# A scan with a mixture of adapters behind it: transposes over 128 rows in place of pairs over 64

## The chip, the cores and the metric

The kernel runs on one core of one Trainium2 chip. The time is the device time of one execution in microseconds; three runs of the kernel before give a median of 207.19 us (206.95 to 208.16). A profile is one execution, taken by the hardware profiler on that core, with every instruction of the five engines (PE, the tensor engine with its weight loads PEld; DVE, the vector engine; ACT, the scalar engine; POOL; SP, which here only issues DMAs) and every DMA packet.

## What is computed

```python
for t in range(S):                      # _attn_ref: a, b are [8, 6400, 128] float32
    h = a[:, t] * h + b[:, t]
    out[:, t] = h
...
logits = x @ w_gate                     # _moe_ref: x is out as [51200, 128]; 8 experts, rank 16
topk = np.argpartition(-logits, K, axis=1)[:, :K]   # K = 2
sel = np.take_along_axis(logits, topk, axis=1)
w = softmax(sel)
for e, k: delta[mask] += w[mask, k, None] * ((x[mask] @ A[e]) @ B[e])
return x + delta
```

A first-order recurrence runs over the tokens, separately for each of 128 channels. Each resulting row then goes through a mixture of eight small adapters, of which the two with the highest logits count.

## The kernel before, in words

The 51200 tokens are cut into 100 chunks of 512 (C = 512, NCH = 100, J = C/128 = 4). A chunk passes through a front and, later, a back.

**Front.** `load` (L526) brings a and b of a chunk with the tokens on the partitions. `front` (L582) transposes them on PE against a float32 identity into PSUM (`trans`, L557, issues at L562), so that the channels lie on the partitions and time along the row: a into `pA`, b into `pB`, two banks each. ACT copies a from PSUM to `a_st` (`add_ae`, L580). DVE runs the recurrence as one TENSOR_TENSOR_SCAN per chunk (L613), reads a_st and pB, and writes the states as float16 to `xT`, of which 24 buffers exist.

**Logits and adapters' first half.** For a unit of six 128-token blocks (`zlogits`, L624) PE multiplies xT by A and w_gate together (L633) into `pZ`, and ACT copies the result to `zl` (L639). **Gating** (`gating`, L645) works on four units, that is six chunks, at once: DVE finds the two largest logits and POOL does the elementwise steps; the last six smaller groups (WIDE_DVE) have all of it on DVE.

**Back** (`back`, L693). zl is multiplied by the gates into `zw`, on POOL at L707 (`mu`) or, for the chunks counted from the end in MU_DVE, on DVE at L711 (`md`). PE transposes zw (L720, float16), the result is copied to `zwT` on DVE (L729) or ACT (L726; `te_act`, L505, chooses), PE adds x and zwT times B in PSUM `pO` (L734 with the identity, L735 with B), ACT copies to `outt` (L744), and `store` (L769) sends two chunks at a time, 512 KB, to HBM. For the last twelve chunks `place` (L752) lets the back use pA and pB too.

**Two kinds of loads.** The first eight chunks (HEAD = 8) come as loads of 256 KB each: a partition gets four tokens, a contiguous 2 KB. `front` transposes such a chunk with four transposes of 128 rows for a (operation A) and four for b (operation B). From chunk 8 on, `paired` (L523) is true: one load of 512 KB brings two chunks, a partition gets eight contiguous tokens, 4 KB, so the first chunk of the pair lies on partitions 0 to 63 and the second on 64 to 127. A chunk's transposes are then over 64 rows, eight per tensor (`pieces`, L547):

```python
dv = dst.rearrange("d (p j) -> d j p", j=HC * J)
lo, hi = 64 * h, 64 * h + 64
return [(dv[:, j, :], t[lo:hi, j, :], ident_f[lo:hi, lo:hi]) for j in range(HC * J)]
```

To use both halves of the array, one operation P joins two such sets on different halves, a of one chunk with b of its neighbour, and alternates them (L592, L597): P of 16 transposes waits for a load of a and a load of b, and for a free bank of each. The load tiles `a_tm` and `b_tm` have six slots of two chunks each.

**Order.** Nothing is a loop at run time. `Program` (L176) gets every operation with an engine, a duration estimate, its dependences and a rank (base by chunk, TEMPLATE by kind, NUDGE by name). `schedule` (L208) simulates the five queues with constants for rates and delays and picks, per engine, from the operations within WINDOW ranks of the first one the one that can start earliest. `waits` (L278) then derives the semaphore waits from the order. All loads but one (b of chunk 0, on ACT) and all stores are issued from SP, in one queue. SPLIT sends two stores (chunks 56 and 78) as two DMAs of 120 and 8 partitions.

Of the kernel before, what the change touches and what calls it, by code (L numbers as in the profile page):

```python
# [15 lines left out]
PE_FREE = 0.1  # L16
Q_RATE = {3: 3.6e-3, 5: 2.1e-3, 7: 2.1e-3}
SCAN_SELF = 0.13
ISSUE = {"sp": 0.52, "act": 0.45}
LOAD_RATE = 392e3  # L20
STORE_RATE = 408e3
# [86 lines left out]
START = (-999, "", 0)  # L108
FIRST = -9999
EARLY = -400  # L110
LEAD = []
TAPER = [2, 2, 1, 1, 1, 1]
WIDE_DVE = [1, 2, 3, 4, 5, 6]
TE_LAST = []
TAIL_UNITS = [4, 4, 4, 4]
TE_ACT = [1]
MU_DVE = [1, 2, 4, 6, 8]
TAIL_CHUNKS = 12
WARM0 = 12
WARM = 16  # L120
HALVES = 0.745
PAIR_RATE = 411e3
HEAD = 8
TAIL = 0
STORE_TAIL = [1, 1, 1, 1]
# [754 lines left out]
```

## Time and profile before

| | us |
|---|---|
| median of three runs | 207.19 (206.95 to 208.16) |
| the profiled execution | 207.91 |
| its span, first to last instruction | 205.9 |
| mean granted clock of PE, share of full | 0.975 |
| DMA: moved, mean over the span | 79.26 MB, 385 GB/s |

The page names a group of instructions by line, engine, operation, and its output and inputs; "x24" is a count, followed by busy us and mean ns of one, then the idle us of the engine just before them and what ended it. In a shape like 64*128 64x64 f32 the first part is the weights' active rows and columns, the second the moving operand. The table by stretch gives the busy us of each engine in each window of time and the number of its instructions there. Matmuls are pipelined, so 0.22 us is the time of one from start to end, and the distance between starts is what it costs in a stream. The groups that the change touches hold, for the whole span:

| group | count, mean ns |
|---|---|
| transposes of 64 rows, L562 | 736 into pA, 736 into pB, 232 each |
| transposes of 128 rows, L562 | 32 into pA, 298; 32 into pB, 290 |
| loads of 512 KB, 4 KB rows | 46 of a, 46 of b; 10.7 and 10.6 us from issue to landing |
| loads of 256 KB, 2 KB rows | 8 of a, 7 of b on SP and 1 on ACT |
| stores of 512 KB, 2 KB rows | 46 |

### The profile page before, as it was taken

How to read it: one execution, taken by the hardware profiler on the slowest of the kernel's cores; microseconds unless marked ns; L12 is line 12 of the kernel's file. 1: busy time of each engine (PE TensorE's matmuls, PEld its weight loads, DVE VectorE, ACT ScalarE, POOL GpSimd, SP SyncE). 2: the span in 40 equal slices, each digit the busy share in tenths (PEclk: the TensorE clock that was granted, in tenths of full speed). 3: DMA queues.
4: the chain of work that ended last, by engine and by line, in shares of the span. 5: the costliest groups of instructions: out<-in, count | busy, mean ns of one | idle time of the engine just before them, and what ended most of it. 6: DMA issues, size and time to landing. Idle time of an engine off the chain costs nothing.

```text
span 205.9 us, 7539 instructions
## 1 busy us (share of the span) xinstructions
PE 184.7 (90%) x3152; PEld 160.9 (78%) x3152; DVE 177.7 (86%) x289; ACT 169.1 (82%) x306; POOL 144.6 (70%) x176
## 2 busy tenths in 40 slices
PE   7779589999998899899799999999999999879683
PEld 6557478887897789788689888988888888857572
DVE  0789688998998899798899999999997999989881
ACT  2356668999998999899799999999999998886372
POOL 1000328879898978878788988899989898687420
PEclk9999958999999999999999999999999999999789
DMA  6999999999999999999999999999999999997388
GB/s 191 368 392 415 405 409 406 405 409 405 411 417 406 414 403 417 409 403 416 408 409 400 409 395 408 415 410 411 409 412 410 410 409 404 405 352 289 132 299 300
DMA packets 30559, 79.26 MB, mean 385 GB/s; under 512 B 3774, under 2 KB 3902, under 8 KB 30526
## 3 DMA queue, kind: packets, MB, share of 16 engines
q1 hardware_dynamic: 29054, 78.39, 97.1%
q10 hardware_dynamic: 1472, 0.40, 0.8%
q8 instruction: 25, 0.41, 0.8%
q14 instruction: 8, 0.07, 0.1%
HBM read 52.56 MB, written 26.21 MB: 383 GB/s over the span
## 4 chain that ended last, share of the span: by engine, by line
PE 67%; DVE 12%; DMA 10%; POOL 3%; issue 3%; SPq 2%; ACT 1%; DVEq 0%; POOLq 0%
PE pA L562 14%; PE pB L562 12%; PE pZ L633 11%; PE pO L734 10%; PE pO L720 10%; PE pO L735 9%; DMA a_tm<-in_a_dram 7%; DVE xT L613 5%; DMA b_tm<-in_b_dram 3%; POOL zw L707 3%; SPq L541 2%; DVE zwT L729 2%; DVE zw L711 1%; ACT outt L744 1%; DVE g L688 1%
## 5 line engine op out<-in xcount | busy, mean ns | idle before, releaser
L613 DVE TENSOR_TENSOR_SCAN xT<-a_st,xT,pB 128x512 f16<-128x512 f32 x96 | 120.3, 1253 | 9.5 <-PE pA L562 5.6
L707 POOL TENSOR_TENSOR zw<-zl,g 128x512 f16<-128x512 f32 x95 | 100.4, 1069 | 24.7 <-PE pO L720 11.3
L562 PE MATMUL pB<-ident_f,b_tm 64*128 64x64 f32 (+1 forms) x768 | 71.4, 235 | 6.5 <-DMA a_tm<-in_a_dram 2.8
L580 ACT COPY a_st<-pA 128x512 f32<-128x512 f32 x100 | 60.5, 612 | 17.5 <-PE pA L562 16.0
L562 PE MATMUL pA<-ident_f,a_tm 64*128 64x64 f32 (+1 forms) x768 | 71.7, 235 | 2.0 <-DMA a_tm<-in_a_dram 1.0
L562 PEld LDWEIGHTS pB<-ident_f,b_tm 64*128 64x128 f32 (+1 forms) x768 | 57.9, 142 | 12.5 <-issue 3.7
L562 PEld LDWEIGHTS pA<-ident_f,a_tm 64*128 64x128 f32 (+1 forms) x768 | 57.9, 142 | 8.2 <-DMA a_tm<-in_a_dram 2.3
L639 ACT COPY zl<-pZ 128x816 f32<-128x816 f32 (+1 forms) x68 | 58.0, 853 | 2.3 <-PE pZ L633 1.6
L744 ACT COPY outt<-pO 128x512 f32<-128x512 f32 x92 | 52.7, 609 | 7.7 <-PE pO L735 7.3
L734 PE MATMUL pO<-ident_h,xT 128*128 128x128 f16 x368 | 50.1, 223 | 1.2 <-DVE zwT L729 1.0
L735 PE MATMUL pO<-cst_h,zwT 128*128 128x128 f16 x368 | 48.9, 220 | 0.8 <-issue 0.8
L734 PEld LDWEIGHTS pO<-ident_h,xT 128*128 128x128 f16 x368 | 40.5, 114 | 4.8 <-DVE zwT L729 2.1
L633 PE MATMUL pZ<-cst_h,xT 128*128 128x136 f16 x400 | 36.5, 228 | 1.5 <-DVE xT L613 0.6
L735 PEld LDWEIGHTS pO<-cst_h,zwT 128*128 128x128 f16 x368 | 36.9, 100 | 0.8 <-issue 0.8
L720 PE MATMUL pO<-ident_h,zw 128*128 128x128 f16 x368 | 33.2, 221 | 2.0 <-ACT outt L744 1.3
L729 DVE COPY zwT<-pO 128x512 f16<-128x512 f16 x77 | 30.2, 410 | 3.4 <-PE pO L720 3.1
L633 PEld LDWEIGHTS pZ<-cst_h,xT 128*128 128x128 f16 x400 | 27.1, 115 | 4.4 <-DVE xT L613 1.3
L720 PEld LDWEIGHTS pO<-ident_h,zw 128*128 128x128 f16 x368 | 22.3, 98 | 6.0 <-issue 1.9
L669 POOL TENSOR_TENSOR k<-zl,m 128x192 f32<-128x192 f32 x15 | 7.8, 519 | 22.9 <-DVE m L667 22.9
L671 POOL TENSOR_SCALAR L<-k 128x192 f32<-128x192 f32 x15 | 12.9, 860 | 1.3
L613 DVE TENSOR_TENSOR_SCAN xT<-a_st,pB 128x512 f16<-128x512 f32 (+1 forms) x8 | 7.5, 939 | 4.6 <-PE pB L562 4.3
L678 POOL TENSOR_TENSOR L<-k,m 128x192 f32<-128x192 f32 x15 | 7.9, 524 | 2.8 <-DVE m L676 2.7
(41 smaller groups left out, 106.1 us busy)
## 6 DMA issues: line engine op xcount, KB each, us to landing
a_tm<-in_a_dram SPq DMA_DIRECT2D x46, 512.0 KB, 10.7
b_tm<-in_b_dram SPq DMA_DIRECT2D x46, 512.0 KB, 10.6
out_dram<-outt SPq DMA_DIRECT2D x46, 512.0 KB, 10.8
a_tm<-in_a_dram SPq DMA_DIRECT2D x8, 256.0 KB, 5.8
b_tm<-in_b_dram SPq DMA_DIRECT2D x7, 256.0 KB, 6.0
out_dram<-outt SPq DMA_DIRECT2D x4, 256.0 KB, 2.7
out_dram<-outt SPq DMA_DIRECT2D x2, 480.0 KB
b_tm<-in_b_dram ACTq DMA_DIRECT2D x1, 256.0 KB, 3.6
```

The costliest lines, as they stand in the source:

```text
L562: last = eng["pe"].transpose(*args)
L580: lambda: eng["act"].copy(a_st[c % NA][:, :], pA[:, c % 2, :]), fr(c, "ae"))
L613: last = eng["dve"].tensor_tensor_scan(out=x[:, s0:s1], data0=a_st[c % NA][:, s0:s1], data1=pB[:, c % 2, s0:s1], initial=init, op0=ALU.mul ...
L633: last = eng["pe"].matmul(pZ[:, k // (n // 2), o : o + W], xblock(b0 + k), Awg_h)
L639: return eng["act"].copy(zl[:, zb : zb + n, :].rearrange("p (h k) w -> p h (k w)", h=2), pZ[:, :, 0 : n // 2 * W])
L671: lambda e: e.tensor_scalar(out=ll, in0=kk, scalar1=0.0, scalar2=-1.0e30, op0=ALU.is_ge, op1=ALU.mult), dve=not main)
L707: lambda: eng["pool"].tensor_tensor(out=wv, in0=zv, in1=gv, op=ALU.mult), ba(gi, c, "mu"))
L720: last = eng["pe"].transpose(ptile[:, k * 128 : k * 128 + 128], zw[w][:, k, :], ident_h[:, :])
L729: lambda: eng["dve"].tensor_copy(zwT[w][:, :], ptile[:, 0:C]), ba(gi, c, "te"))
L734: eng["pe"].matmul(dst, xblock(b0 + k), ident_h[:, :], start=True, stop=False)
L735: last = eng["pe"].matmul(dst, zwT[w][:, k * 128 : k * 128 + 128], B_h, start=False, stop=True)
L744: lambda: eng["act"].copy(outt[:, o0 : o0 + n, :].rearrange("p k w -> p (k w)"), bank),
```

## The change

HEAD goes from 8 to 4, and a new list FLAT names the pairs 2 to 49, that is every chunk from 4 on. `paired` is false for them. Their loads are still 512 KB for two chunks, but arranged as the single ones were: each partition gets four tokens of the first chunk and four of the second, two runs of 2 KB. So every chunk lies on all 128 partitions, and every chunk is transposed as the first eight were: four transposes of 128 rows for a (operation A) and four for b (operation B), as separate operations with waits of their own. No P operation is left. In the tail, MU_DVE goes from five of the last eight chunks to all of the last ten, so five more products move from POOL to DVE; TE_LAST, empty before, names six of the last ten chunks whose zwT copy moves from DVE to ACT. SPLIT becomes empty, so no store is cut. All ranks are new (TEMPLATE, NUDGE, WINDOW), the planner's rates are slightly different, and it counts two margins for the order alone: 2.0 us for what SP waits for and 1.0 us behind a DMA.

```diff
-LOAD_RATE = 392e3
-STORE_RATE = 408e3
+SP_MARGIN = 2.0
+LAND_MARGIN = 1.0
+LOAD_RATE = 387e3
+STORE_RATE = 413e3
...
-WINDOW = {'pe': 16.262, 'act': 17.153, 'dve': 47.02, 'pool': 47.064, 'sp': 57.831}
+WINDOW = {'pe': 70.239, 'act': 22.0, 'dve': 48.055, 'pool': 40.461, 'sp': 37.357}
...
-TE_LAST = []
+TE_LAST = [1, 2, 4, 6, 8, 10]
+HEAD_UNITS = []
+FLAT = [2, 3, 4, ..., 49]
-MU_DVE = [1, 2, 4, 6, 8]
+MU_DVE = [1, 2, 3, 4, 5, 6, 7, 8, 9, 10]
-PAIR_RATE = 411e3
-HEAD = 8
+PAIR_RATE = 414.5e3
+HEAD = 4
-SPLIT = {56: [120, 8], 78: [120, 8]}
+SPLIT = {}
...
+    def margin(self, d, op):
+        return (SP_MARGIN if op.eng == "sp" else 0.0) + (LAND_MARGIN if d.sem is not None else 0.0)
...
-                users[d.i].append((op, self.lag(d, op)))
+                users[d.i].append((op, self.lag(d, op) + self.margin(d, op)))
...
         def paired(c):
-            return HEAD <= c < NCH - TAIL
+            return HEAD <= c < NCH - TAIL and c // HC not in FLAT
...
-                    q, f"{key}{c}", n * C * D * 4 / (PAIR_RATE if paired(c) else LOAD_RATE),
+                    q, f"{key}{c}", n * C * D * 4 / (PAIR_RATE if paired(c) else STORE_RATE if n == HC else LOAD_RATE),
```

The NUDGE and TEMPLATE tables, all of whose numbers differ, are left out, as are changes that have no effect with these settings (HEAD_UNITS is empty).

More of the change, by code (lines that the diff above doesn't have):

```diff
@@ L113 @@
 WIDE_DVE = [1, 2, 3, 4, 5, 6]
-TE_LAST = []
+TE_LAST = [1, 2, 4, 6, 8, 10]
 TAIL_UNITS = [4, 4, 4, 4]
+HEAD_UNITS = []
+FLAT = [2, 3, 4, 5, 6, 7, 8, 9, 10, 11, 12, 13, 14, 15, 16, 17, 18, 19, 20, 21, 22, 23, 24, 25, 26, 27, 28, 29, 30, 31, 32, 33, 34, 35, 36, 37, 38, 39, 40, 41, 42, 43, 44, 45, 46, 47, 48, 49]
 TE_ACT = [1]
-MU_DVE = [1, 2, 4, 6, 8]
+MU_DVE = [1, 2, 3, 4, 5, 6, 7, 8, 9, 10]
 TAIL_CHUNKS = 12
@@ L121 @@
 HALVES = 0.745
-PAIR_RATE = 411e3
-HEAD = 8
+PAIR_RATE = 414.5e3
+HEAD = 4
 TAIL = 0
 STORE_TAIL = [1, 1, 1, 1]
-SPLIT = {56: [120, 8], 78: [120, 8]}
+SPLIT = {}
 TEMPLATE = {
-    "la": [-13.284, -13.376, -10.147],
-    "lb": [-12.856, -11.393, -13.112],
-    "A": [3.619, 4.619, -4.264, 6.619, 7.619, 8.619],
-    "B": [-2.245, 2.718, -8.407, 8.99, 6.061, 4.41],
-    "ae": [-1.493, 12.357, 10.831, 7.96, 5.931, 11.772],
-    "sc": [-2.149, -1.286, 6.521, -19.69, -9.638, -0.216],
-    "Z": [6.623, 2.916, -2.696, 9.959],
-    "ze": [6.413, 12.686, 18.636, 4.611],
-    "g1": [1.078],
-    "g2": [15.192],
-    "g3": [12.311],
-    "g4": [-7.624],
-    "g5": [43.586],
-    "g6": [18.91],
-    "w1": [27.261],
+    "la": [-17.155, -9.476, -8.608],
+    "lb": [-13.364, -10.414, -12.68],
+    "A": [16.518, 7.296, 8.525, 9.015, 10.156, 14.759],
+    "B": [6.922, 7.465, 8.658, 10.963, 11.979, 21.937],
+    "ae": [-7.077, -3.484, 19.127, 16.938, 8.043, 17.193],
+    "sc": [12.365, 35.856, 12.744, 17.786, 39.079, 14.296],
+    "Z": [-3.119, 5.335, 10.342, 12.093],
+    "ze": [8.877, 13.518, 17.919, 16.392],
+    "g1": [12.118],
+    "g2": [-0.105],
+    "g3": [10.708],
+    "g4": [15.86],
+    "g5": [12.078],
+    "g6": [28.459],
+    "w1": [12.393],
     "w2": [27.183],
@@ L146 @@
     "p3": [35.473],
-    "mu": [22.377, 11.789, 38.051, -6.995, 25.901, 25.822],
-    "T": [17.564, 18.694, 15.643, 19.013, 20.568, 20.925],
-    "te": [11.47, 21.167, 12.791, -1.785, 1.996, 11.732],
-    "D": [13.525, 17.402, 15.169, 14.035, 19.652, 27.901],
-    "oe": [26.926, 32.894, 33.316, 36.556, 35.829, 26.06],
-    "st": [25.679, 26.621, 29.881],
-    "ta": [14.725, 30.746, 16.943, 18.052, 19.161, 20.27],
-    "md": [78.718, -0.018, -87.87, 12.1, 13.209, 14.318],
+    "mu": [-6.716, -6.575, 22.528, 27.11, 24.647, 25.876],
+    "T": [22.12, 19.993, 15.194, 8.772, -12.047, 12.625],
+    "te": [11.32, 58.704, 8.268, 34.31, 22.158, 22.327],
+    "D": [21.417, 22.577, 2.823, -5.791, 8.081, -5.073],
+    "oe": [23.904, 20.839, 22.806, 31.415, 27.39, 36.64],
+    "st": [23.265, 25.145, 26.221],
+    "ta": [17.267, 11.772, 45.843, 23.351, 24.128, 24.904],
+    "md": [3.609, 47.296, 8.162, 22.686, 23.463, 24.239],
     "wu": [-0.198],
-    "ch": [26.813],
+    "ch": [-35.18],
     "mb": [0.0],
-    "q2": [17.668],
-    "q3": [-16.399],
-    "q5": [-0.842],
-    "q6": [-2.93],
-    "q7": [1.928],
+    "q2": [-17.861],
+    "q3": [-7.73],
+    "q5": [3.392],
+    "q6": [14.473],
+    "q7": [-2.223],
     "q8": [35.473],
-    "g7": [47.426],
-    "g8": [9.111],
+    "g7": [15.59],
+    "g8": [17.3],
 }
@@ L348, in bass_associative_scan_2x2__then__mixture_of_adapters_kernel @@
     b0 = 0
-    for n in [U] * ((NBLK - sum(TAIL_UNITS)) // U) + TAIL_UNITS:
+    for n in HEAD_UNITS + [U] * ((NBLK - sum(HEAD_UNITS) - sum(TAIL_UNITS)) // U) + TAIL_UNITS:
         units.append((b0, n))
@@ L513, in un @@
         def un(u, kind):
-            return (PERIOD * (u // GMAX), kind, u % GMAX)
+            v = u - len(HEAD_UNITS)
+            if v < 0:
+                return ((units[u][0] + units[u][1] - 1) // J - 1, kind, 0)
+            return (sum(HEAD_UNITS) // J + PERIOD * (v // GMAX), kind, v % GMAX)
         def ga(gi, kind):
@@ L721, in tr @@
                 return last
-            o_T[c] = P.add("pe", f"T{c}", 0.1 + 0.056 * n, [(o_mu[c], True), (o_ih, True)] + free + [(o, True) for o in o_wu if c < 2], tr, ba(gi, c, "T"))
+            o_T[c] = P.add("pe", f"T{c}", 0.1 + 0.056 * n, [(o_mu[c], True), (o_ih, True)] + free + [(o, True) for o in (o_wu if c < 2 else [])], tr, ba(gi, c, "T"))
             if te_act(c):
```

159 rows, old and new, of the table NUDGE are left out of this document.

## The prediction

> **What bounds the kernel now.** I read the page first: its busy shares, its 40 slices and its chain.
>
> ```profile
> span 205.9 us, 7539 instructions
> PE 184.7 (90%) x3152; PEld 160.9 (78%) x3152; DVE 177.7 (86%) x289; ACT 169.1 (82%) x306; POOL 144.6 (70%) x176
> PE   7779589999998899899799999999999999879683
> DVE  0789688998998899798899999999997999989881
> PEclk9999958999999999999999999999999999999789
> DMA  6999999999999999999999999999999999997388
> PE 67%; DVE 12%; DMA 10%; POOL 3%; issue 3%; SPq 2%; ACT 1%; DVEq 0%; POOLq 0%
> ```
>
> DMA is full from 5 to about 187 us, yet the chain that ended last runs through PE for 67% of the span and through DMA for 10%. So the transfers are busy but early; the compute engines, PE ahead, pace the middle. How tightly, the table by stretch says (busy us of PE, PEld, DVE, ACT, POOL; then clock, DMA share, GB/s), with the row of the tile pA alone (PE, PEld, DVE, ACT) under it:
>
> ```profile
> 30.00:180.00 150.00, 144.14 (x2679) 127.27 (x2677) 139.41 (x210) 139.33 (x252) 129.76 (x155) 0.99 1.03 409
> 162.20:172.20 10.00, 10.00 (x196) 8.96 (x194) 9.65 (x15) 9.63 (x18) 9.61 (x12) 1.00 1.04 411
> 180.00:190.00 10.00, 8.25 (x121) 6.71 (x119) 8.94 (x30) 7.24 (x15) 7.47 (x8) 1.00 0.89 332
> 190.00:200.00 10.00, 7.69 (x97) 6.91 (x94) 8.35 (x31) 5.29 (x14) 3.62 (x3) 0.83 0.53 197
> ...
> 30.00:180.00 150.00, 60.08 (x672) 48.83 (x672) 0.00 (x0) 50.17 (x83) 0.99 1.03 409
> ```
>
> The last row counts 83 evacuations of a on ACT in 150 us: one chunk per 1.81 us. In the second row PE has no gap; the groups of PE in that stretch show what a chunk costs it there:
>
> ```profile
> L562 PE MATMUL pA<-ident_f,a_tm 64*128 64x64 f32 x48 | 4.3, 229 | 0.0
> L734 PE MATMUL pO<-ident_h,xT 128*128 128x128 f16 x24 | 3.4, 222 | 0.0
> ```
>
> 48 half transposes of a, eight to a chunk, are six chunks in 10 us (and 24 matmuls with ident_h, four to a chunk, are six as well): 1.67 us each when PE runs without a gap, against 1.81 on average. PE has a few per cent of slack in the middle, no more.
>
> **The change, part by part.** *1. Transposes over 128 rows.* Every chunk from 8 on loses 16 transposes of 64 rows and gets 8 of 128 rows. The timeline of PE shows one paired operation between its neighbours (start, duration), and, from the first 20 us, transposes over 128 rows:
>
> ```profile
> 162.25 0.52 PE L633 MATMUL pZ<-cst_h,xT 128*128 128x136 f16 x6
> 162.60 0.22 PE L734 MATMUL pO<-ident_h,xT 128*128 128x128 f16 x1
> ...
> 162.99 0.22 PE L735 MATMUL pO<-cst_h,zwT 128*128 128x128 f16 x1
> 163.14 0.27 PE L562 MATMUL pA<-ident_f,a_tm 64*128 64x64 f32 x1
> ...
> 163.63 0.22 PE L562 MATMUL pA<-ident_f,a_tm 64*128 64x64 f32 x1
> 163.79 0.55 PE L633 MATMUL pZ<-cst_h,xT 128*128 128x136 f16 x6
> ```
>
> ```profile
> 10.01 0.60 PE L562 MATMUL pA<-ident_f,a_tm 128*128 128x128 f32 x4
> 10.86 0.66 PE L562 MATMUL pB<-ident_f,b_tm 128*128 128x128 f32 x4 [0.25 <-DMA b_tm<-in_b_dram]
> 16.85 0.55 PE L633 MATMUL pZ<-cst_h,xT 128*128 128x136 f16 x6
> 17.23 0.39 PE L483 MATMUL pO<-ident_f 128*128 128x128 f32 x2
> ```
>
> Paired: D's eight matmuls start from 162.60 to 162.99, a step of 0.39/7 = 0.056 us, but from the last of them to the first half transpose (163.14) it is 0.15, so entering costs 0.095. From 163.14 to the next operation at 163.79 it is 0.65. Together 0.745 us per chunk. Over 128 rows: four last 0.60 us and the last of them 0.27, so the step is 0.33/3 = 0.11 and a tensor's four take 0.437 (0.109 each before rounding); two tensors 0.874. The difference is +0.129 us per chunk, the lower end if A and B enter for nothing. Entering is not quite free: six logits matmuls that step to D in 0.35 (162.25 to 162.60) step to a 128-row f32 transpose in 0.38 (16.85 to 17.23), and a group that had waited takes 0.66 instead of 0.60. With 0.03 for each of the two visits it is +0.19, the upper end. Which visits follow one another the trace of before cannot show; I take +0.15, nearer the lower end because A and B stand side by side or follow a ready neighbour when PE is the late engine.
>
> [...]
>
> *The middle, 30 to 180 us.* The clock around its start, by stretch, and PE's work in it by groups:
>
> ```profile
> 22.60:26.00 3.40, 1.68 (x38) 1.45 (x38) 1.63 (x2) 1.57 (x4) 1.98 (x3) 1.00 1.02 408
> 26.00:33.00 7.00, 6.54 (x82) 5.49 (x82) 5.67 (x8) 4.96 (x8) 3.04 (x4) 0.51 1.03 408
> ```
>
> ```profile
> L562 PE MATMUL pB<-ident_f,b_tm 64*128 64x64 f32 x680 | 60.5, 230 | 2.3 <-issue 2.0
> L562 PE MATMUL pA<-ident_f,a_tm 64*128 64x64 f32 x672 | 60.1, 231 | 0.9 <-issue 0.9
> L734 PE MATMUL pO<-ident_h,xT 128*128 128x128 f16 x324 | 43.4, 222 | 0.4 <-DVE zwT L729 0.3
> L633 PE MATMUL pZ<-cst_h,xT 128*128 128x136 f16 x353 | 31.7, 226 | 0.6 <-DVE xT L613 0.3
> L720 PE MATMUL pO<-ident_h,zw 128*128 128x128 f16 x326 | 29.0, 220 | 0.8 <-POOL zw L707 0.5 <-ACT outt L744 0.2
> ```
>
> By steps: 1352/16 = 84.5 chunks x 0.745 = 63.0; L734 with L735 (as many), 648 x 0.0557 = 36.1; L633, 353 x 0.35/6 = 20.6; L720, of the same shape as L734, 326 x 0.0557 = 18.2; and 1.4 because the clock is at half from 26 to 32.9 us (0.51 over 7 us). Sum 139.3, so PE is truly free for 10.7 of the 150 us. The change adds 84.5 x 0.15 = 12.7 (10.9 to 16.1): it fills all of PE's slack and more. The stretch gets longer by 139.3 + 12.7 + the waits that stay - 150. Waits: none stay at best (the gapless 10 us show that PE can), all 10.7 at worst; I take 3, nearer the gapless row, because DVE and ACT at 139 of 150 would then be the ones that wait. That is **+5.0 us** (ends +0.2 and +16.1).
>
> *2. One chunk and one tensor at a time.* A paired operation waits for two loads and two free banks and holds PE's queue until the last of them; A and B each wait for one. That doubles the waits on PE, priced above, and lets ACT's copy of a start before b has landed. New ranks and planner constants move order only; their effect is the waits that stay, 0 to 10.7.
>
> *3. Loads: 512 KB with 2 KB rows.* Stores are already 512 KB with 2 KB rows, the early 256 KB loads have 2 KB rows, the others 4 KB. Three stretches by the table (the last number is GB/s), the first store (outt) and the last load (b_tm) in the timeline of SP, and how long loads take to land (us, median):
>
> ```profile
> 8.00:14.00 6.00, 4.42 (x33) 3.43 (x32) 5.08 (x5) 2.66 (x5) 0.00 (x0) 1.00 1.05 389
> 15.50:38.00 22.50, 19.01 (x304) 15.97 (x304) 18.52 (x20) 16.65 (x28) 9.58 (x12) 0.85 1.02 407
> 175.00:179.00 4.00, 3.80 (x73) 3.46 (x72) 3.80 (x14) 3.57 (x7) 2.32 (x3) 1.00 1.06 407
> 38.18 0.40 SPq L779 DMA_DIRECT2D out_dram<-outt  x1
> 161.92 0.47 SPq L541 DMA_DIRECT2D b_tm<-in_b_dram  x1
> b_tm<-in_b_dram SPq DMA_DIRECT2D x46, 512.0 KB, 10.6
> ```
>
> The first store is issued at 38.18, so 15.5 to 38 is loads of 4 KB rows alone; the last load, issued at 161.92, has landed by about 173 to 175, so 175 to 179 is stores of 2 KB rows alone: both 407 GB/s. So I take 0 for the row length. The other bound is 389, the small loads: 524288 bytes take 1.348 instead of 1.288 us, +0.06 x 96 loads = 5.8 us of DMA. Its cover is the DMA's idle share between 180 and 200 us (332 and 197 of 409 GB/s, 7.1 us idle), so even that adds little while compute ends last. A gain is possible only at the first chunks, where eight 256 KB loads become four: 8 x 262144 bytes at 389 against 407 is 0.24 us.
>
> *4. Head.* Chunk 4 now waits for two 512 KB loads instead of two of 256 KB, about 1.3 us later. PE and DVE wait there anyway (digits 7, 7, 7, 9, 5 and 0, 7, 8, 9, 6), and the few chunks from 8 on that are transposed before 30 us (100, less the 83 of the middle and those after it, less the first eight) find the same cover: 0. SP issues four loads and two split stores fewer; it was never the late one: 0.
>
> *5. Tail.* Five more products of the last ten chunks go from POOL to DVE, six copies of zwT from DVE to ACT:
>
> ```profile
> L711 DVE TENSOR_TENSOR zw<-zl,g 128x512 f16<-128x512 f32 x5 | 3.3, 682 | 0.0
> L729 DVE COPY zwT<-pO 128x512 f16<-128x512 f16 x9 | 3.8, 417 | 1.0 <-PE pO L720 1.0
> L707 POOL TENSOR_TENSOR zw<-zl,g 128x512 f16<-128x512 f32 x10 | 11.1, 1125 | 6.6 <-PE pB L720 4.0 <-PE pO L720 1.7 <-PE pA L720 0.9
> ```
>
> DVE: 5 x 0.682 - 6 x 0.417 = +0.9 us on an engine busy 17.3 of 20 us there; ACT's six copies lie in its free time (12.5 of 20 busy). But each product takes 0.68 instead of 1.12 before its transposes can start, up to 0.44 less on a chain. Between -0.4 and +0.9 I take **+0.5**: DVE is the busiest engine there.
>
> **Sum.** +5.0 + 0.5 = +5.5. The profiled execution took 207.91 (span 205.9 and 2.0 around it), so it would take 213.4; it stood 0.7 above the median of 207.19, so I forecast 212.7.
>
> **Rivals.** *(a) The slack absorbs it.* The lower price (+10.9) meets 10.7 of slack and nothing of it is kept: the middle stays at 150 us, about 207.4. [...] Against: it needs PE without a gap for 150 us, which the trace has in single stretches.
>
> *(b) Faster: the half-clock stretch does not come.* In the clock's rows above, after 3.4 us in which PE was busy for half, its clock is at half for about 6.8 us, worth 3.4 us of work. Transposes over 128 rows fill more of the early time; if the stretch does not come and PE's price is the lower one, it is 207.2 - 3.4 = 203.8. It decides as soon as the middle costs less than 1.3 us. Against: PE waits for data there, and dearer transposes do not end such waits. [...]
>
> *(c) Heavier.* Every visit pays and the waits stay: +16.1 + 0.5 is 223.8; with half of the waits, 139.3 + 16.1 + 5.3 - 150 + 0.5 = +11.2, 218.4.
>
> **How the numbers follow.** A measurement of this kernel can tell 1% (2.1 us) from no change. Forecast 0.55 (its own range 209.5 to 217), (a) 0.17, (b) 0.17, (c) 0.11. So faster 0.17, same 0.17, slower 0.66. The range reaches down to (b), 203.5, and up to the lighter form of (c), 218.5; about 0.15 is left out.
>
> **What would show it.** Right: 800 transposes of a and b, steps of 0.109 us, PE at 9 in all slices from 30 to 180 us, chunks 1.83 to 1.9 us apart by ACT's copies, waits of DVE, ACT and POOL on PE grown, GB/s below 409 in the middle. Wrong: chunks still 1.81 apart or less (a, b); loads alone at 389 GB/s; a clock of 1.00 from 20 to 34 us (b); a new stretch at half clock, or a tail after the last scan of more than 20 us, which no term above holds.

## The result, and the profile after

| | before | after |
|---|---|---|
| median (lowest to highest), us | 207.17 (206.02 to 208.16), 9 runs | 209.04 (208.83 to 209.17), 9 runs |
| the profiled execution, us | 207.91 | 208.98 |
| its span, us | 205.9 | 207.1 |

The ratio is 1.0091, with a 95% interval of 1.0068 to 1.0114. The change makes the kernel 0.9% slower: 1.9 us, where +5.5 was forecast. The time lies inside the stated range, but the rise is a third of the one forecast, and what follows shows that it has another cause.

The page of the kernel after, in the lines that answer to those shown of before:

```profile
span 207.1 us, 6052 instructions
PE 192.9 (93%) x2416; PEld 181.5 (88%) x2416; DVE 177.2 (86%) x288; ACT 172.6 (83%) x312; POOL 138.3 (67%) x171
PE   7888899999999999999969998999999998998972
DVE  0669898999998989899859988898889889999990
PEclk9999999999999999999999999999999999999999
DMA  7999999999999999999999999999999999999868
PE 60%; DMA 23%; DVE 10%; SPq 4%; issue 1%; ACT 1%; DVEq 0%
...
a_tm<-in_a_dram SPq DMA_DIRECT2D x48, 512.0 KB, 11.4
```

PE's share rises as forecast, but in the chain that ended last PE falls from 67% to 60% and DMA rises from 10% to 23%. A load takes 11.4 us from issue to landing where it took 10.7. In this execution the clock is full everywhere (1.00 on average): the stretch at half clock is gone. The table by stretch of the kernel after (busy us of PE, PEld, DVE, ACT, POOL; clock, DMA share, GB/s), and the row of the tile pA alone under it (PE, PEld, DVE, ACT):

```profile
15.50:38.00 22.50, 21.00 (x232) 19.28 (x233) 20.55 (x26) 18.63 (x33) 12.29 (x16) 1.00 1.05 386
20.00:30.00 10.00, 8.94 (x95) 8.20 (x93) 9.02 (x12) 7.55 (x14) 6.57 (x9) 1.00 1.05 386
30.00:180.00 150.00, 146.62 (x1928) 142.84 (x1926) 135.33 (x194) 134.31 (x241) 124.57 (x151) 1.00 1.05 397
40.00:100.00 60.00, 60.00 (x797) 58.69 (x796) 55.85 (x79) 55.90 (x102) 53.05 (x64) 1.00 1.05 398
100.00:180.00 80.00, 76.62 (x1004) 74.43 (x1003) 70.27 (x103) 69.45 (x125) 64.16 (x77) 1.00 1.05 397
180.00:185.00 5.00, 4.80 (x61) 4.22 (x58) 4.71 (x10) 4.61 (x9) 3.35 (x4) 1.00 1.05 405
190.00:200.00 10.00, 9.13 (x133) 7.57 (x132) 10.00 (x46) 8.41 (x19) 0.00 (x0) 1.00 0.81 302
```

```profile
30.00:180.00 150.00, 47.37 (x316) 34.22 (x316) 0.00 (x0) 47.21 (x80) 1.00 1.05 397
```

Loads alone (15.5 to 38) run at 386 GB/s, where before had 407. From 40 to 100 us PE is busy in 60.00 of 60, and over the 150 us of the middle the chunks come 150/80 = 1.875 us apart instead of 1.81. The tempting reading is that PE sets this pace. The DMA share of 1.05 beside it says that the DMA engines are full as well; which of the two does it, the page cannot say. The experiments do.

What one chunk costs PE, in the timeline of PE after:

```profile
60.20 0.39 PE L735 MATMUL pO<-ident_h,zw 128*128 128x128 f16 x4
60.43 0.61 PE L577 MATMUL pA<-ident_f,a_tm 128*128 128x128 f32 x4
60.87 1.04 PE L577 MATMUL pB<-ident_f,b_tm 128*128 128x128 f32 x8
61.74 0.22 PE L749 MATMUL pO<-ident_h,xT 128*128 128x128 f16 x1
...
62.64 0.52 PE L648 MATMUL pZ<-cst_h,xT 128*128 128x136 f16 x6
62.99 0.60 PE L577 MATMUL pA<-ident_f,a_tm 128*128 128x128 f32 x4
```

Four transposes over 128 rows take 0.44 us, start to start (60.43 to 60.87), eight take 0.87 (60.87 to 61.74), and entering from float16 work costs nothing here (60.20 to 60.43 is 0.23 for four float16 transposes, their usual step). The price is the lower end, +0.129 us per chunk. With the 0.90 of two chunks' sums in pO (61.74 to 62.64) and the 0.35 of the logits of a chunk and a half, a chunk needs 0.87 + 0.45 + 0.23 + 0.23 = 1.78 us of PE. Over the middle the chunks come 1.875 apart, so PE has 5% to spare there. The spare time is not spread evenly: from 40 to 100 us, 797 matmuls at 24 a chunk (8 transposes, 4 each of the other four kinds) are 33.2 chunks, 1.81 us apart, so PE has about 2% to spare; its gaps come from 100 to 180 us, where it is busy in 76.62 of 80.

The end of the run, by the last scan on DVE and the last copy to outt on ACT, before and then after:

```profile
185.34 1.27 DVE L613 TENSOR_TENSOR_SCAN xT<-a_st,xT,pB 128x512 f16<-128x512 f32 x1
201.88 1.17 ACT L744 COPY outt<-pB 128x512 f32<-128x512 f32 x2 [1.11 <-PE pB L735]
```

```profile
187.82 1.26 DVE L628 TENSOR_TENSOR_SCAN xT<-a_st,xT,pB 128x512 f16<-128x512 f32 x1
203.95 0.58 ACT L759 COPY outt<-pB 128x512 f32<-128x512 f32 x1 [0.21 <-PE pB L750]
```

With the landing of the last load, taken from the traces, the runs can be cut in the same pieces (us); e5 and e8 are missing, because their profiled executions were slow ones (spans of 386.8 and 320.5 us), and of e8's only the rate of the loads alone is read.

| kernel | last load landed | to the end of the last scan | to the end of the last copy | span |
|---|---|---|---|---|
| before | 174.6 | 12.0 | 16.4 | 205.9 |
| after | 180.8 | 8.3 | 15.4 | 207.1 |
| e1: after, 4 KB rows | 174.7 | 8.0 | 15.4 | 201.1 |
| e3: after, fewer transposes | 180.7 | 8.3 | 15.4 | 207.6 |
| e13: after, 4 KB rows and fewer transposes | 173.9 | 8.4 | 15.4 | 201.2 |
| e2: before, 2 KB rows | 180.4 | 10.2 | 14.9 | 209.7 |
| e4: before, fewer transposes | 174.1 | 10.3 | 14.9 | 202.4 |
| e7: before, last pair early | 174.8 | 7.4 | 24.0 | 210.4 |
| e9: before, PE kept busy | 174.8 | 10.2 | 16.4 | 204.2 |
| e14: before, tail engines | 174.4 | 12.3 | 15.0 | 205.0 |
| e15: before, both | 174.8 | 10.3 | 15.0 | 203.1 |
| e10: pairs in after's order | 176.2 | 8.0 | 15.4 | 202.6 |

The last load lands 6.2 us later, and the drain behind it, down to the end of the span, is 26.3 us instead of 31.3: 3.7 of the 5.0 between landing and last scan, 1.0 between last scan and last copy. The sum is +1.2 us of span (+1.1 in the time of the two profiled executions; before's stood 0.7 above its median).

### The profile page after: what moved, and what is told of

Read it like the earlier page. It is cut to its first block, busy times and chain, and to the rows that moved or that the text cites. A ratio compares the mean times of both kernels' runs of the same rounds, so it can differ in the third digit from the quotient of the medians.

```text
span 207.1 us, 6052 instructions
## 1 busy us (share of the span) xinstructions
PE 192.9 (93%) x2416; PEld 181.5 (88%) x2416; DVE 177.2 (86%) x288; ACT 172.6 (83%) x312; POOL 138.3 (67%) x171
## 4 chain that ended last, share of the span: by engine, by line
PE 60%; DMA 23%; DVE 10%; SPq 4%; issue 1%; ACT 1%; DVEq 0%
DMA a_tm<-in_a_dram 17%; PE pA L577 16%; PE pB L577 15%; PE pZ L648 8%; PE pO L735 7%; PE pO L749 7%; PE pO L750 7%; DMA b_tm<-in_b_dram 6%; SPq L556 4%; DVE zw L726 3%; DVE zwT L744 2%; DVE xT L628 2%; DVE L L689 1%; ACT outt L759 1%; DVE L L693 0%
## 5 line engine op out<-in xcount | busy, mean ns | idle before, releaser
L722 POOL TENSOR_TENSOR zw<-zl,g 128x512 f16<-128x512 f32 x90 | 94.8, 1062 | 23.4 <-DVE g L703 11.1
L595 ACT COPY a_st<-pA 128x512 f32<-128x512 f32 x100 | 58.5, 603 | 14.2 <-PE pA L577 12.9
L577 PE MATMUL pA<-ident_f,a_tm 128*128 128x128 f32 x400 | 59.7, 276 | 4.2 <-DMA a_tm<-in_a_dram 4.0
L577 PE MATMUL pB<-ident_f,b_tm 128*128 128x128 f32 x400 | 60.3, 276 | 1.4 <-DVE xT L628 0.6
L759 ACT COPY outt<-pO 128x512 f32<-128x512 f32 x92 | 51.4, 598 | 9.1 <-PE pO L750 8.4
L577 PEld LDWEIGHTS pA<-ident_f,a_tm 128*128 128x128 f32 x400 | 43.7, 142 | 6.2 <-DMA a_tm<-in_a_dram 6.0
L749 PE MATMUL pO<-ident_h,xT 128*128 128x128 f16 x368 | 47.8, 220 | 0.6 <-DVE zwT L744 0.5
L577 PEld LDWEIGHTS pB<-ident_f,b_tm 128*128 128x128 f32 x400 | 43.4, 141 | 3.7 <-DMA b_tm<-in_b_dram 2.3
L648 PE MATMUL pZ<-cst_h,xT 128*128 128x136 f16 x400 | 35.0, 223 | 0.7 <-DVE cst_h L499 0.6
L735 PEld LDWEIGHTS pO<-ident_h,zw 128*128 128x128 f16 x368 | 24.3, 97 | 3.5 <-issue 0.9
## 6 DMA issues: line engine op xcount, KB each, us to landing
a_tm<-in_a_dram SPq DMA_DIRECT2D x48, 512.0 KB, 11.4
```

The costliest lines, as they stand in the source:

```text
L577: last = eng["pe"].transpose(*args)
L595: lambda: eng["act"].copy(a_st[c % NA][:, :], pA[:, c % 2, :]), fr(c, "ae"))
L648: last = eng["pe"].matmul(pZ[:, k // (n // 2), o : o + W], xblock(b0 + k), Awg_h)
L722: lambda: eng["pool"].tensor_tensor(out=wv, in0=zv, in1=gv, op=ALU.mult), ba(gi, c, "mu"))
L735: last = eng["pe"].transpose(ptile[:, k * 128 : k * 128 + 128], zw[w][:, k, :], ident_h[:, :])
L749: eng["pe"].matmul(dst, xblock(b0 + k), ident_h[:, :], start=True, stop=False)
```

## The experiments

**1. Rows of the loads, or PE: e1, e3, e13 and e2.** Two theories stood for the later landing. PE theory: dearer transposes free the load tiles later, and SP's loads wait for them. DMA theory: loads in rows of 2 KB are slower in themselves. e1 takes the rows back (a load of two chunks is again one run of 4 KB per partition), e3 takes PE work away, e13 does both, and e2 gives the kernel before the rows of 2 KB. The first three are edits of the kernel after.

```diff
 e1:
-                if paired(c):
+                if n == HC:
 e3 (e13 has both edits):
-                return [(dv[:, j, :], t[:, h * J + j, :], ident_f[:, :]) for j in range(J)]
+                return [(dv[:, j, :], t[:, h * J + j, :], ident_f[:, :]) for j in range(J if c < 16 else 3)]
 e2, in the kernel before:
-                if paired(c):
+                if paired(c) and n != HC:
```

e1:


> The changed kernel with one thing put back: its 512 KB loads have 4 KB rows again (eight consecutive tokens to a partition). Instructions, waits and order of every engine are those of the changed kernel; only the tokens of a pair come out interleaved, so the output is a recurrence over another order of the tokens. DMA theory (rows of 2 KB make each load 0.07 us longer, 96 loads, and the transfers, full until 195 us, set the end): loads alone back at 407 GB/s in place of 386, the middle at 409 in place of 397, and 203 to 206 us. PE theory (0.129 us more of transposes per chunk sets the pace, the transfers lie beside them): 208 to 209.2 us, with the waits for a_tm gone and nothing else moved.

Measured: 202.88 us, ratio to before 0.9771 (0.9757 to 0.9784), that is 6.2 us less than the median of the kernel after. Its table by stretch, and the last scan and the last copy:

```profile
15.50:38.00 22.50, 21.62 (x242) 19.91 (x241) 21.02 (x28) 19.14 (x34) 13.03 (x18) 1.00 1.03 408
40.00:100.00 60.00, 60.00 (x797) 58.69 (x795) 55.86 (x80) 55.90 (x101) 52.90 (x64) 1.00 1.03 412
100.00:180.00 80.00, 80.00 (x1070) 78.56 (x1069) 74.24 (x114) 73.06 (x133) 67.69 (x81) 1.00 1.03 410
```

```profile
181.41 1.27 DVE L628 TENSOR_TENSOR_SCAN xT<-a_st,xT,pB 128x512 f16<-128x512 f32 x1
197.53 0.58 ACT L759 COPY outt<-pB 128x512 f32<-128x512 f32 x1 [0.21 <-PE pB L750]
```

PE, DVE and ACT do the same work in 40 to 100 us, to within 0.01 us; there only GB/s differs, 412 against 398. The difference in pace comes behind that: from 100 to 180 us the kernel after has gaps on PE (1004 matmuls) and e1 has none (1070). The last load lands 6.1 us earlier, and the last scan and the last copy come 6.4 us earlier.

e3:


> The changed kernel with three of four transposes per tensor from chunk 16 on (the fourth is left out, so a quarter of each such chunk is stale): PE loses 0.218 us per chunk, 84 chunks, order and waits as they are. PE theory: the pace falls to what DVE and ACT allow, below 1.78 us per chunk, 202 to 205 us. DMA theory: the loads still come at 386 to 397 GB/s, 208 to 209 us.

Measured: 209.47 us, ratio 1.0089 (1.0074 to 1.0103): a quarter of the transposes gone from chunk 16 on, 84 x 2 x 0.109 = 18 us of PE, and no gain; the last load lands at 180.7 us, as in the kernel after (180.8).

e13:


> Both edits: 4 KB rows and three of four transposes from chunk 16 on (tokens interleaved, a quarter stale). DMA theory: as with 4 KB rows alone, 203 to 206 us. PE theory: as with three of four alone, 202 to 205 us. If the two bind together, each alone gives less than 2 us and this one 6 us or more, to 203 us or below.

Measured: 203.0 us, ratio 0.9785 (0.9769 to 0.98), the same as e1. The rows of e3 and of e13 from 40 to 100 us:

```profile
40.00:100.00 60.00, 57.97 (x740) 51.75 (x738) 56.74 (x80) 56.38 (x102) 53.75 (x65) 1.00 1.05 398
```

```profile
40.00:100.00 60.00, 57.71 (x738) 51.36 (x736) 56.77 (x83) 56.19 (x102) 53.83 (x65) 1.00 1.03 412
```

The rate follows the rows of the loads and not PE's work. The PE theory falls: a PE busy in 60.00 of 60 us did not pace the kernel. What sets the pace of the chunks within these 60 us stays open, as it hardly moves with either: 33.2 chunks in the kernel after and in e1, and in e3 and e13, at 22 matmuls a chunk, 33.6 and 33.5.

e2:


> The kernel before with one thing changed: its 512 KB loads have 2 KB rows (four tokens of each of two chunks to a partition); transposes, waits and order as before (tokens of a pair come out interleaved, so the recurrence runs over another order). DMA theory: loads alone at 386 GB/s in place of 407, 46 x 2 loads 0.07 us longer, 6.4 us of transfers of which the idle end of the queue can take some: 210 to 213 us. PE theory, and the prediction's own term of 0 for the row length: 207 us, within 1.

Measured: 212.04 us, ratio 1.0216 (1.0199 to 1.0234), +4.4 against the 207.6 of the kernel before in the same session. Loads alone are at 386 again, now with transposes over 64 rows:

```profile
15.50:38.00 22.50, 18.69 (x318) 15.69 (x318) 19.00 (x21) 17.29 (x29) 9.72 (x13) 0.92 1.05 386
```

**2. What a row costs: e8.**

```diff
-                    view = src[r0 : r0 + n * C, :].rearrange("(h p j) d -> p h j d", p=128, j=J)
+                    view = src[r0 : r0 + n * C, :].rearrange("(h p j) d -> p h j d", p=128, j=J if c < HEAD else 2)
...
```

> The changed kernel with its 512 KB loads in rows of 1 KB (four runs per partition of two blocks each) in place of 2 KB; the transposes and the order stay. Tokens of a chunk come out in another order, which changes no time. Theory (each further row of a load costs its DMA engine a fixed time, and the loads set when the front ends): the step from 4 KB to 2 KB rows, 8 to 16 rows for each of 16 engines, made a load 0.07 us longer, so the step to 32 rows makes it another 0.14 us longer: loads alone near 350 GB/s, the last load lands some 13 us later than in the changed kernel, and the time is near 222 us. Rival (a load of more than one run per partition costs something once, whatever its rows): loads alone stay near 386 GB/s and the time stays near 209 us.

Measured: 222.26 us, ratio 1.0712 (1.0669 to 1.0756). The rate of its loads alone, from an execution in which PE's clock was at 0.56 while the DMA share was 1.09:

```profile
15.50:38.00 22.50, 22.37 (x148) 19.07 (x147) 15.68 (x17) 13.12 (x21) 7.96 (x10) 0.56 1.09 348
```

Three points lie on one line: 524288 bytes take 1.285 us at 408 GB/s, 1.358 at 386 and 1.507 at 348. From 8 to 16 to 32 rows for each of 16 DMA engines that is 9.1 and 9.3 ns per further row, an estimate that takes the rows as spread evenly over the engines. The third point rests on that one execution, but the times agree with it: 96 loads that are each 0.149 us longer make 14.3 us, and 13.2 were measured against the kernel after. The rival, that the second run costs once, falls.

**3. Why the drain is shorter: e4, e7, e5, e9, e14, e15.**

e4 takes PE work from the kernel before (`range(HC * J)` in pieces becomes `range(HC * J if c < 16 else 6)`).

> The kernel before with six of eight half transposes per tensor from chunk 16 on (a quarter of each such chunk is stale); order, waits and loads as before. PE loses 4 steps of 0.061 us in 84 chunks, 0.12 us per chunk, as much as the change added to it. If PE paces the kernel before, as the prediction said, the middle gets up to 10 us shorter and the kernel 3 to 8 us faster. If the transfers set its middle, 207 us, within 1.

Measured: 204.79 us, ratio 0.9901 (0.9864 to 0.9937): 2.4 us, neither the large gain nor nothing. With a quarter of its transposes gone, before's front is 10.3 us behind the last load instead of 12.0, and from the last scan to the last copy it is 14.9 us instead of 16.4. There PE's lateness counted, but for about 2 us only. The half clock from 26 to 33 us is still there (0.54).

e7 moves the front's last pair ahead in the kernel before (`ae98`, `ae99` behind `ze64` on ACT, `sc98` and `sc99` earlier on DVE).

> The kernel before with four operations earlier in their engine's order and nothing else changed: ACT's copies of a for chunks 98 and 99 directly behind the logits copy that follows their transposes, and DVE's two last scans before the rest of the gating that stands ahead of them. Tail-order theory (the changed kernel with 4 KB rows is 4.7 us faster than before because the last pair, landed at 174.6, goes through the front at once instead of 6 us later): 2 to 4 us faster, 203.5 to 205.5. Tail-engine theory (the gain is the products and copies that changed engines): within 1 of 207.

Measured: 211.6 us, ratio 1.0194 (1.0148 to 1.0241). The last scan does end earlier, 7.4 us behind the last load, but from it to the last copy it is 24.0: what the scans overtook is late instead. PE's clock also fell there (0.60 from 185 to 190 us, where before has 1.00; over the whole execution 0.965 instead of 0.975), so how much is the order and how much the clock is not shown. In this order, at least, a shorter way to the last scan was worth nothing.

e5 is e1 with the tail's five products on POOL and the six copies on DVE again, each at the place of its planned time.

> The changed kernel with 4 KB rows (202.9 us, tokens of a pair interleaved) and the tail's engines of before: five products back from DVE to POOL and six copies of zwT back from ACT to DVE, each put into its new engine's order at the time at which the plan had it; all else keeps its order. Tail-engine theory: most of the 4.7 us is lost again, 206 to 208 us. Tail-order theory: 202.5 to 204.5. The prediction's own term for this part, +0.5 us for the move, would make it 202.4.

Measured: 205.24 us, ratio 0.9922 (0.9897 to 0.9948), 2.4 us above e1 by the medians and 3.1 by the ratios. That lies between the two ranges expected: half to two thirds of the 4.7 us is lost. A lower clock does not explain it: the runs with a mean clock of 0.995 to 1.0 take 204.97 to 205.75 us, and e1 took 202.74 to 202.92 at 0.996 to 0.997.

e9 puts work into PE's early idle time in the kernel before; the other two are the mirror of e5, and both together.

```diff
         P.schedule()
+        FILL = {"Z3": 14, "Z4": 7}
+        for name, n in FILL.items():
+            order = P.order["pe"]
+            i = next(i for i, o in enumerate(order) if o.name == name) + 1
+            for k in range(n):
+                op = P.add("pe", f"f{name}_{k}", 0.109, [], lambda: eng["pe"].transpose(pO[:, 0, 0:128], ident_f[:, :], ident_f[:, :]), START)
+                order.insert(i + k, op)
...
```

> The kernel before with 21 transposes of the identity put into PE's order where PE had been idle between 21.9 and 26.4 us (14 behind the fourth Z, 7 behind the fifth), so that PE is never half idle there. Clock theory (the stretch at half clock that follows those idle times delays the back, and the end with it): the half-clock stretch is gone, the first copy of pO to outt comes some 2 to 4 us earlier, and the kernel is 2 to 4 us faster, 203 to 205 us. Rival (loads set the front's end all the same, and what the back loses at 26 to 33 us it makes up later in PE's slack): within 1 us of the kernel before, whatever the clock.

Measured: 206.0 us, ratio 0.994 (0.9914 to 0.9966): 1.4 us less by the medians, 1.2 by the ratio. The clock, by the row that had 0.51 before:

```profile
26.00:33.00 7.00, 6.01 (x112) 4.78 (x111) 6.81 (x10) 5.95 (x10) 3.56 (x5) 1.00 1.03 408
```

The mechanism is right, the size smaller than the 2 to 4 us expected, as is the first copy to outt (35.2 us instead of 36.5, 1.3 earlier): matmuls that compute nothing save time, and the clock stays up in this stretch. The front is then 10.2 us behind the last load instead of 12.0, and the last load lands when it did.

e14 (TO_DVE = [3, 5, 7, 9, 10] for the products, TO_ACT = [1, 2, 4, 6, 8, 10] for the copies, counted from the end):

> The kernel before with the changed kernel's tail engines alone: of the last 12 chunks, five products go from POOL to DVE and six copies of zwT from DVE to ACT, each at the place of the order that its planned time gives. Theory (the tail's engines are worth 2.4 us of the drain, as taking them back in the variant with 4 KB rows showed): 204 to 205.5 us, the last load lands where it did, and the drain is 28 to 29 us. Rival (they are worth it only with the order that was searched for them): 207 us or more.

Measured: 206.29 us, ratio 0.9942 (0.9916 to 0.9969). From the last scan to the last copy it is 15.0 us instead of 16.4; the rest stays. The median is 1.1 us lower, less than the 2.4 that e5 lost, and between the ranges of the theory and the rival. Which of the two moves gives it was not tried apart, and the traces hold another reading. From 190 to 200 us PE's clock was 0.83 in the kernel before and is 1.00 here. The same row of e9, of e4 and of e14:

```profile
190.00:200.00 10.00, 8.41 (x103) 7.45 (x104) 8.20 (x32) 5.18 (x12) 2.02 (x2) 0.83 0.65 243
190.00:200.00 10.00, 7.12 (x105) 5.94 (x104) 7.52 (x31) 6.23 (x14) 1.34 (x2) 1.00 0.77 287
190.00:200.00 10.00, 7.89 (x122) 6.67 (x120) 9.10 (x36) 9.12 (x21) 0.00 (x0) 1.00 0.69 255
```

Where this clock is 0.83 (before, e9) the last copy comes 16.4 us behind the last scan; where it is 1.00 it comes 14.9 behind in e4, which keeps the tail's engines of before, and 15.0 in e14. So whether the moved work itself shortens the tail here, or a clock that did not fall, is not shown.

e15:


> The kernel before with both of its drain's repairs: the 21 transposes of the identity in PE's early idle time, and the changed kernel's tail engines at planned places. Theory (the two act at different places, the first on how far the front is behind the last load, 12.0 us to 10.2, the second on the time from the last scan to the last copy to outt, 16.5 us to 15.0): they add, 1.2 and 1.2 us, so 204.7 to 205.2 us, with 8 and more us less drain at neither place. Rival (both only remove the same lateness of the tail): 206 us, as each alone.

Measured: 204.64 us, ratio 0.986 (0.9839 to 0.9881). By the medians the two add, 3.0 us against 1.4 and 1.1 alone: 10.3 us to the last scan as in e9, 15.0 to the last copy as in e14. All of the reference is computed here, and it is 1.4% faster than before. Its last scan and last copy:

```profile
183.82 1.27 DVE L617 TENSOR_TENSOR_SCAN xT<-a_st,xT,pB 128x512 f16<-128x512 f32 x1
198.94 1.19 ACT L753 COPY outt<-pB 128x512 f32<-128x512 f32 x2
```

**4. The order without the rows: e10.** FLAT is cut to pairs 40 to 49, so 4 KB rows and pairs of 64 rows hold from chunk 4 to chunk 79. The changed kernel's order is written into the kernel as a list for each engine, which is not shown here.

```diff
-FLAT = [2, 3, 4, ..., 49]
+FLAT = list(range(2, 2)) + list(range(40, 50))
...
```

> The changed kernel with pairs of 64 rows and loads of 4 KB rows again from chunk 4 to chunk 79, 2 KB rows and transposes over 128 rows for chunks 80 to 99, and its new tail engines; the order is the changed kernel's own, with each paired operation at the place of the later of its two halves. All of the reference is computed. Theory (rows of loads set the front's end, the order and the tail engines the drain): 76 loads are 0.07 us shorter, 5.3 us, so the last load lands near 175.5, the drain stays at 26 us, and the time is 203 to 204.5 us. Rival (the shorter drain needs transposes of one tensor at a time, which let the back start early): the drain goes back to 29 to 31 us and the time is 206 to 208 us.

Measured: 204.4 us, ratio 0.9857 (0.9835 to 0.9879), with all of the reference computed: faster than both kernels. Loads of 4 KB rows run at 407 GB/s, as in the kernel before, and the drain is the changed kernel's, 8.0 and 15.4 us:

```profile
15.50:38.00 22.50, 20.39 (x348) 17.33 (x348) 20.35 (x24) 18.48 (x31) 12.28 (x16) 0.85 1.03 407
26.00:33.00 7.00, 6.20 (x114) 5.33 (x114) 6.36 (x10) 6.39 (x12) 6.83 (x9) 1.00 1.03 407
```

In the second row POOL is busy 6.83 of 7 us, where before had 3.04: the back begins earlier in this order (first copy to outt at 29 us, 36 before). Its clock was at half for as long as before's, only earlier (0.54 from 17 to 24 us, and 0.85 over 15.5 to 38 as before), and the last scan is still only 8.0 us behind the landing. So the short drain comes with the order and the tail's engines; it does not need transposes of one tensor at a time before chunk 80. The last twenty chunks keep them here, and were not tried without.

## Why the prediction was right or wrong

The direction was right, by another cause than the forecast gave, and two large terms that it did not have nearly cancel: the last load lands 6.2 us later, and the drain behind it is 5.0 us shorter. That their difference is a small rise, inside the stated range, is luck.

*Transposes over 128 rows, +0.15 per chunk: right in size, wrong in worth; the step to +5.0 us failed.* The price is +0.129, the lower end (the stretch shown has no extra 0.03 per entry). But the step that made it +5.0 us, PE's need set against PE's time in the middle, assumed that PE paces the middle, and that the transfers are "busy but early". The runs show 0 in its place in the changed kernel: e3 and e13 take 18 us off PE and gain nothing, and e1, which pays the price and has the rows of before, takes as many chunks through the 150 us of the middle as before did (83). In the order of before PE's work counts for a little: e4 took off about the price and gained 2.4 us. A gapless stretch of 10 us of PE was read as the bound of the 150, of which PE's steps fill only 139.3 by the forecast's own sum. The premise came from the chain of before, where PE had 67%: such a chain follows who released whom, and it can stay on PE through the buffers of the load tiles, although the loads, in a queue that is full from 5 us to the last landing (a DMA share of 1.03 from 30 to 180 us), fix when the front can end: e1 and e2 move the last landing by the rows alone, by 6.1 and 5.8 us.

*Loads with 2 KB rows, 0: this step failed.* The forecast took the stores' rate (407) for the loads'. It named the other bound from the right row, loads of 256 KB at 389 GB/s, and what it gives: +0.06 x 96 = 5.8 us. Measured: 6.2 us between before and after, 6.1 between e1 and after, 5.8 between e2 and before. The reason for calling it covered, idle DMA between 180 and 200 us, was wrong too: idle DMA behind the last load covers nothing that lies before it, as the drain only starts when the load has landed. The 407 was not firm for the stores either: alone, from 180 to 185 us, they run at 405 GB/s in the kernel after and at 390 in e1.

*Head, 0.* No run has it alone; but rival (b)'s mechanism lives there. Its half-clock stretch did not come in the profiled execution (clock 1.00 from 20 to 30 us, where before had 0.51 from 26 to 33). The rival gave it 3.4 us, all of it at the end; e9 shows 1.2 to 1.4 us in the kernel before, and where the rest went is not shown. In the kernel after a somewhat lower clock seems to cost nothing: four of its nine runs have a mean clock of 0.987 or 0.988, and they take 208.83 to 209.17 us, as the others do (208.94 to 209.12); where in those runs the clock was low is not shown.

*Tail, +0.5: wrong in sign.* The value was taken from DVE's sum (+0.9), as the busiest engine there. e14 shows -1.1 us in the order of before, where the clock behind 190 us may be what gives it, and e5 -2.4 in the changed kernel's order: the other end of that term, -0.4 for products off POOL, was the nearer one.

*Together:* +6.2 for the landing, -3.7 on the way to the last scan, -1.0 from there to the last copy, -0.3 for what follows it. The sum is +1.2 us of span. The first term is shown, by one edit each way (e1, e2). How the drain's 5.0 us divides among causes is not. About 1.8 of the 3.7 can be had in the kernel before without its new order: from a clock that stays up (e9, 12.0 to 10.2), from less PE work with the half clock left in place (e4, 10.3), or with slower loads, where less of the clock was lost too (e2, 10.2; 0.92 over 15.5 to 38 us instead of 0.85). But e10, in the new order and with as long a time at half clock, has the whole of it (8.0), so the new order can do it without the clock. What in the order does it, the earlier back or something else, and why the tail's engines are worth 2.4 us in one order and at most 1.1 in another, stays open. Rival (a), that the slack absorbs PE's price, was right about PE. Rival (c) is refuted.

## What to carry to other kernels

Look for the queue that is never empty until the last input has landed: what lengthens each of its transfers moves the last landing by most of the sum (6.1 us of 96 x 0.073 = 7.0 between e1 and the kernel after), however busy another engine looks, while work taken from a full engine that only keeps up with it gains nothing (18 us of it in e3) or little (2.4 us in e4). Cut the run at the last landing and account for both sides separately; a term that is covered behind the landing is not covered before it. And take a transfer's rate from rows of the same direction: a store's rate need not be a load's (with rows of 2 KB, stores alone ran at 390 to 407 GB/s here and loads alone at 386).

## What the runs showed of the hardware

- Each further row of a load costs about 9 ns on one of 16 DMA engines, an estimate from three rates with the rows spread evenly: loads alone run at 408, 386 and 348 GB/s with rows of 4, 2 and 1 KB. Stores alone, with 2 KB rows, ran at 407 (before), 405 (after) and 390 (e1); no run gave them another row, so what a row costs a store is not shown.
- Two idle times of PE, 1.95 and 0.89 us long, were followed by half the clock for 6.8 us (0.51 over 26 to 33 us); with 21 transposes of the identity in PE's order there it stayed at 1.00 (e9). The rows of the kernel before in which they end:

```profile
23.89 0.27 PE L562 MATMUL pB<-ident_f,b_tm 64*128 64x64 f32 x1 [1.95 <-DMA a_tm<-in_a_dram]
26.46 0.36 PE L562 MATMUL pB<-ident_f,b_tm 64*128 64x64 f32 x1 [0.89 <-DMA a_tm<-in_a_dram]
```

- Pairs over 64 rows save less than their step says: eight pairs step by 0.061 us, 0.49 in all, eight transposes over 128 rows by 0.109, 0.874; but entering and leaving the pairs takes 0.255 of the 0.385 us between them, by the one paired operation that was timed.
